# Decode attention with a gated MLP on one core: the value products one tile behind the scores instead of two, with the value tiles loaded one iteration earlier

## The chip, the core and the metric

The kernel runs on one core of a Trainium2 chip. The core's engines run side by side, each through its own list of instructions in order: TensorE (PE, with its weight loads shown as PEld), VectorE (DVE), ScalarE (ACT), GpSimd (POOL) and SyncE (SP). In this kernel SP does one thing: it issues the loads, one after the other, and where a load has to wait for a buffer, every load behind it on SP waits too. The loads run on 16 DMA engines. The metric is the time of one execution in microseconds, lower being better.

## The reference

One decoding step of a transformer block, for 4 sequences of one new token each, width 512, in bf16. Cut to what matters:

```python
x = A_x                                          # (4, 1, 512)
sa, ca, ga, sb, cb, gb = (silu(c) @ w_mod) in 6 parts
h = layernorm(x) * (1 + ca) + sa
q = (h @ wq), 32 heads of 128                    # one query per head and sequence
scores = q . k_cache * 128 ** -0.5               # k_cache: (4, 32, 4096, 128)
o = softmax(scores) . v_cache                    # v_cache: (4, 32, 4096, 128)
x = x + ga * (o @ wo)
h = layernorm(x) * (1 + cb) + sb
x = x + gb * gated_mlp(h)                        # w_in 512 x 1792, gelu, layernorm, gate, w_out 896 x 512
```

Both caches together have 268 MB, and every element is used once. The profile counts 282.73 MB read.

## The kernel before

**Tiles.** The work on the caches is cut into 32 tiles, i = 0 to 31 (the code calls the last one `L`). Tile i is a group g = i // 4 of four heads and a sequence b = i % 4: 4 heads x 4096 keys x 128 numbers, 4096 KB of keys and as much of values. On the chip a tile is 128 partitions x 128 keys x 128 numbers; 32 partitions belong to a head. We write K(i) and V(i) for the loads of its keys and values.

**What one tile needs.** For the scores, DVE multiplies the keys by the query, in two halves of 64 keys per partition (`mult`, L278, written in place into the key tile `kt`). PE adds up groups of 8 products by sixteen matmuls with the identity (`reduce_d`, L284, into `red`), and DVE adds up what is left (`sum8`, L293). `scores` (L298) finishes the second half, finds the maximum over DVE (L302 to L309) and lets ACT take the exponentials (L316), one instruction per head, into one of three buffers `pbd`; the sums come out beside them. `norm_r`, `norm_a` and `norm_b` (L324, L331, L340 or L344) turn these sums into reciprocals: one DVE instruction, one matmul with ones in fp32, which is two passes on PE, and a DVE reciprocal.

The value products are `pv` (L353): 32 matmuls of `pbd` with the value tile `vt` into `ops`, one of two PSUM tiles. `o_pick` (L361, L365) brings the four useful blocks of `ops` together by four DVE instructions, `o_cols` (L375 or L379) turns the result into columns by small matmuls, and `o_scale` (L395) multiplies by the reciprocal. After every fourth tile `project` lets PE multiply by `wo` (`o_proj`, L405), and `add_up` adds the result to `acc` on DVE (L413). The last tile's values go another way, `o_last` (L389): its key tile's shape lets single columns of `pbd` be used, and no `o_pick` is needed.

**Order.** Everything is in the order in which it is written; nothing is planned by a scheduler. Iteration i of the main loop (L433) works on the scores of tile i: `mult(i, 0)`, then `scores(i - 1)`, the norm and the extraction of earlier tiles, `reduce_d(i, 0)`, `mult(i, 1)`, `reduce_d(i, 1)`, and at its end the value products of tile i - 2. The extraction (`o_pick`, `o_cols`, `o_scale`) belongs to tile i - 3. After the loop stand the softmax of tile 31, the extraction of tile 29, the value products and the extraction of tile 30, the projection of tiles 28 to 30, then `o_last`, the second layernorm and the MLP. Of the layernorm and the MLP's first matmul most is done for all columns before the last tile's part is known; the last column is put in behind.

**Buffers and the queue.** `kt` and `vt` have two buffers each. K(i + 2) takes K(i)'s buffer, so its load waits until `reduce_d(i, 1)` has read it; it is issued in iteration i (L455). V(i) takes V(i - 2)'s buffer and is issued at the end of iteration i, behind `pv(i - 2)` (L464 to L466). V(31) takes a key buffer, that of K(30), and comes in four pieces (64, 32, 16 and 16 keys); K(31) comes in two halves. All of these go through SP's queue, with w_mod and wq ahead of them, wo_sb and wo_last issued in iteration 2, and win_sb and wout_sb, the MLP's weights, behind V(31). So the order of the loads is: w_mod, wq, K(0), K(1), V(0), K(2), V(1), K(3), K(4), V(2), wo, K(5), V(3), and so on to K(30), V(28), K(31), V(29), V(30), V(31), win_sb, wout_sb.

The functions that the change touches and what calls them, with the line numbers of the profile:

Of the kernel before, what the change touches and what calls it, by code (L numbers as in the profile page):

```python
# [22 lines left out]
def kernel(  # L23
# [34 lines left out]
    L = NT - 1  # L58
# [12 lines left out]
    def ps_sm(shape, dtype=F32):  # L71
        return psum.tile(shape, dtype, name="sm", bufs=3)
# [18 lines left out]
    def kv_view(cache, i):  # L91
        g, b = divmod(i, B)
        v = cache[b, g * HQ:(g + 1) * HQ].rearrange("h s d -> (h s) d")
        return v.rearrange("(p n) d -> p n d", p=P)
# [3 lines left out]
    def load(dst, src, cuts):  # L98
        n0 = 0
        for n in cuts:  # L100
            nc.sync.dma_start(out=dst[:, n0:n0 + n, :], in_=src[:, n0:n0 + n, :])
            n0 += n
# [6 lines left out]
    def load_v(i):  # L109

        vts[i] = kvp.tile([P, NJ, DH], BF16, name="kt" if i == L else "vt", bufs=2)
        load(vts[i], kv_view(A_v_cache, i), TAIL if i == L else (NJ,))
# [162 lines left out]
    def mult(i, kc):  # L275
        kt = kts[i][:, kc * KC:(kc + 1) * KC, :]
        g, b = divmod(i, B)
        nc.vector.tensor_tensor(out=kt, in0=kt, in1=bc(qbc[:, g, b, :], KC), op=ALU.mult)  # L278
# [19 lines left out]
    def scores(i):  # L298
        sum8(i, 1)
        S = st.pop((i, "S"))  # L300
        mrow = wk.tile([P, 1], F32, name="mrow")
        nc.vector.tensor_reduce(out=mrow, in_=S, axis=AX.X, op=ALU.max)  # L302
        mb = wk.tile([P, R], F32, name="mb")
        nc.vector.tensor_copy(out=mb, in_=mrow.to_broadcast([P, R]))  # L304
        mt = wk.tile([P, R], F32, name="mt")
        nc.vector.transpose(mt, mb)  # L306
        nM = wk.tile([P, 1], F32, name="nM")
        nc.vector.tensor_reduce(out=nM, in_=mt, axis=AX.X, op=ALU.max)  # L308
        nc.vector.tensor_scalar(  # L309
            out=nM, in0=nM, scalar1=-att_scale, scalar2=None, op0=ALU.mult  # L310
        )
        pbd = pbds[i % 3]
        rs = wk.tile([P, 1], F32, name="rs", bufs=3)
        for q in range(HQ):
            r = slice(R * q, R * (q + 1))
            nc.scalar.activation(  # L316
                out=pbd[r, :, q], in_=S[r, :], func=AF.Exp, bias=nM[r, :],
                scale=att_scale, accum_out=rs[r, :],
            )
        st[i, "rs"] = rs  # L320
# [27 lines left out]
    def pv(i):  # L348

        for m in range(NJ // G):  # L350
            n = slice(m * G, (m + 1) * G)
            g = R * (m % 4)
            nc.tensor.matmul(  # L353
                opss[i % 2][g:g + G * HQ], lhsT=pbds[i % 3][:, n, :], rhs=vts[i][:, n, :],
                start=(m < 4), stop=(m >= NJ // G - 4), tile_position=(0, g),
            )

    def o_pick(i):
        ops = opss[i % 2]
        osb = wk.tile([P, DH], F32, name="osb")  # L360
        nc.vector.tensor_scalar(  # L361
            out=osb, in0=ops[:, 0, :], scalar1=selg[:, 0:1], scalar2=None, op0=ALU.mult
        )
        for g in range(1, G):
            nc.vector.scalar_tensor_tensor(  # L365
                out=osb, in0=ops[:, g, :], scalar=selg[:, g:g + 1], in1=osb,
                op0=ALU.mult, op1=ALU.add,
            )
        st[i, "osb"] = osb

    def o_cols(i):
        op = ps_sm([P, 2, 2])
        osb = st.pop((i, "osb"))
        if i // B == NQ - 1:
            nc.tensor.matmul(op, lhsT=osb, rhs=sel4, start=True, stop=True)  # L375
        else:
            for a in range(2):
                for r in range(2):
                    nc.tensor.matmul(  # L379
                        op[64 * a:64 * (a + 1), r, :], lhsT=osb[:, r:P:2],  # L380
                        rhs=sel4[:, a:HQ:2], start=True, stop=True, tile_position=(0, 64 * a),
                    )
        st[i, "op"] = op
# [10 lines left out]
    def o_scale(i):  # L394
        nc.vector.tensor_tensor(  # L395
            out=oTs[:, i], in0=st.pop((i, "op")), in1=st.pop((i, "rz")), op=ALU.mult
        )

    def o_proj(g, b0, b1):
        wp = ps_sm([P, DJ, b1 - b0])  # L400
        for j in range(DJ):
            for q in range(HQ):
                r, t = divmod(q, 2)
                w = wo_last[:, q, :] if g == NQ - 1 else wo_sb[:, g * 2 + t, r, :]
                nc.tensor.matmul(  # L405
                    wp[:, j, :], lhsT=w[:, j:D:DJ], rhs=oTs[:, g * B + b0:g * B + b1, r, t],
                    start=(q == 0), stop=(q == HQ - 1),
                )
        return wp
# [13 lines left out]
    def project(i):  # L423

        if i >= 0 and i % B == BL and i < L:
            adds.append((o_proj(i // B, 0, B), 0, B))
# [6 lines left out]
    for i in range(NT):  # L433
        more = list(QPLAN.get(i, ()))
        mult(i, 0)
        if i >= 1:
            scores(i - 1)
        if i >= 2:
            norm_b(i - 2)
        add_up()  # L440
        if i >= 3:
            o_pick(i - 3)
        reduce_d(i, 0)
        if i >= 3:
            o_cols(i - 3)
        if more:
            queries(more.pop(0))
        mult(i, 1)
        if i >= 1:
            norm_r(i - 1)  # L450
        if i >= 3:
            o_scale(i - 3)
        sum8(i, 0)
        reduce_d(i, 1)
        load_k(i + 2)  # L455
        if i >= 1:
            norm_a(i - 1)
        project(i - 3)
        while more:
            queries(more.pop(0))  # L460
        if i >= 2:
            pv(i - 2)
        if i == 0:
            load_v(1)  # L464
        elif 2 <= i < L:
            load_v(i)  # L466
        if i == 2:
            nc.scalar.dma_start(out=sp_t[:, 0:1], in_=B_w_sp[0:1, 0:1])
            nc.scalar.dma_start(out=sp_t[:, 1:2], in_=B_b_sp.rearrange("(a b) -> a b", b=1))
            mps = ps_sm([P, 3 * DJ, B])  # L470
            mod_cols(2, 3 * DJ, mps)
            nc.vector.tensor_copy(out=modT, in_=mps)
            nc.vector.tensor_copy(out=hcs[:, :, B:2 * B], in_=mps[:, DJ:2 * DJ, :])
            gps = ps_sm([P, P])
            for k in range(DJ):
                for j in range(DJ):
                    nc.tensor.matmul(
                        gps[R * j:R * (j + 1), :], lhsT=cTw[:, k, :],
                        rhs=wm_sb[:, k, 5 * D + j * P:5 * D + (j + 1) * P],
                        start=(k == 0), stop=(k == DJ - 1), tile_position=(0, R * j),  # L480
                    )
            nc.vector.tensor_copy(out=gbr, in_=gps)
            pre_cm.__exit__(None, None, None)
            wts = tl = ctx.enter_context(tc.tile_pool(name="wts", bufs=1))
            wo_sb = wts.tile([P, H // 2 - 2, 2, D], BF16, name="wo_sb")
            wo_last = wts.tile([P, HQ, D], BF16, name="wo_last")
            hl = (H - HQ) * DH
            nc.sync.dma_start(
                out=wo_sb, in_=A_wo[0:hl].rearrange("(t p r) n -> p t r n", p=P, r=2)
            )  # L490
            nc.sync.dma_start(out=wo_last, in_=A_wo[hl:H * DH].rearrange("(q p) n -> p q n", p=P))
        if i == 5:
            sps = ps_sm([P, 2])
            nc.tensor.matmul(sps, lhsT=ones_b, rhs=sp_t, start=True, stop=True)
            nc.vector.tensor_copy(out=spf, in_=sps)
            for k, t in ((0, gbw), (1, gbr)):
                nc.vector.tensor_scalar(
                    out=t, in0=gbr, scalar1=spf[:, k:k + 1], scalar2=None, op0=ALU.mult
                )
            cbT = modT[:, 2 * DJ:3 * DJ, :]  # L500
            nc.vector.tensor_scalar_add(out=cbT, in0=cbT, scalar1=1.0)
        if i == L - 1:
            load_v(L)
            win_sb = wts.tile([P, DJ, F], BF16, name="win_sb")
            nc.sync.dma_start(out=win_sb, in_=B_w_in.rearrange("(p j) n -> p j n", p=P))
            wout_sb = wts.tile([P, NH, D], BF16, name="wout_sb")
            nc.sync.dma_start(out=wout_sb, in_=B_w_out.rearrange("(j p) n -> p j n", p=P))
# [3 lines left out]
    norm_b(L - 1)  # L511
    norm_r(L)
    add_up()
    o_pick(L - 2)
    o_cols(L - 2)
    norm_a(L)
    o_scale(L - 2)
    norm_b(L)
    pv(L - 1)
    o_pick(L - 1)  # L520
    o_cols(L - 1)
    o_scale(L - 1)
# [141 lines left out]
```

## Time and profile before

| what | value |
|---|---|
| median of 3 runs | 675.5 us (673.76 to 675.64) |
| the profiled execution | 673.46 us, its span 671.7 us |
| mean granted clock of TensorE | 0.823 |
| PE busy | 405.1 us (60%) |
| DVE busy | 423.3 us (63%) |
| ACT busy | 85.0 us (13%) |
| HBM read | 282.73 MB, 421 GB/s over the span |
| one multiply of half a key tile on DVE (L278) | 4420 ns |
| one set of 16 matmuls of `reduce_d` | 3.61 us at full clock, 5.04 to 6.56 us where it begins at half clock |

How to read it: the page gives busy times by engine, and cuts the span into 40 slices of 16.8 us, with the busy share of each engine and of the DMA engines in tenths, the granted clock of TensorE (PEclk) and the GB/s moved. "Chain that ended last" follows the work back from the last instruction, at each step to what released it; its shares sum to the span. A row of the timeline has the start and the duration in us, the engine (SPq is a DMA issue on SP), the line, the operation, what it writes and reads, the number of instructions that it merges, and in brackets the idle time of the engine before it with what ended it. Rows of the DMA view end with the median time from the issue of a load to its landing. A row of the windows view has the stretch, its length, the busy time of each engine asked for with its number of instructions, the granted clock, the busy share of the DMA engines and the GB/s.

### The profile page before, as it was taken

How to read it: one execution, taken by the hardware profiler on the slowest of the kernel's cores; microseconds unless marked ns; L12 is line 12 of the kernel's file. 1: busy time of each engine (PE TensorE's matmuls, PEld its weight loads, DVE VectorE, ACT ScalarE, POOL GpSimd, SP SyncE). 2: the span in 40 equal slices, each digit the busy share in tenths (PEclk: the TensorE clock that was granted, in tenths of full speed). 3: DMA queues.
4: the chain of work that ended last, by engine and by line, in shares of the span. 5: the costliest groups of instructions: out<-in, count | busy, mean ns of one | idle time of the engine just before them, and what ended most of it. 6: DMA issues, size and time to landing. Idle time of an engine off the chain costs nothing.

```text
span 671.7 us, 7155 instructions
## 1 busy us (share of the span) xinstructions
PE 405.1 (60%) x2971; PEld 183.0 (27%) x2971; DVE 423.3 (63%) x620; ACT 85.0 (13%) x278; POOL 3.3 (0%) x15
## 2 busy tenths in 40 slices
PE   1185784466577655555666566666556457755766
PEld 1032332222223222222222222223222223322325
DVE  3176593775666777566577666666776566777733
ACT  1012120111011111101111110111111011111112
POOL 1000000000000000000000000000000000000000
PEclk9998988677888777889867777887777898777975
DMA  9999999999999999999999999999999999999994
GB/s 375 437 431 433 422 410 422 434 427 426 434 432 428 433 430 427 434 435 428 426 432 431 435 430 431 425 431 432 432 430 435 426 430 433 433 426 426 436 414 168
DMA packets 13556, 283.19 MB, mean 422 GB/s; under 512 B 1228, under 2 KB 2644, under 8 KB 4692
## 3 DMA queue, kind: packets, MB, share of 16 engines
q1 hardware_dynamic: 13488, 282.73, 98.5%
q8 instruction: 23, 0.38, 0.2%
q14 instruction: 9, 0.07, 0.0%
q10 hardware_dynamic: 36, 0.01, 0.0%
HBM read 282.73 MB, written 0.00 MB: 421 GB/s over the span
## 4 chain that ended last, share of the span: by engine, by line
DMA 53%; DVE 31%; PE 14%; issue 1%; ACT 0%; SPq 0%; DVEq 0%
DMA kt<-in_A_k_cache_dram 53%; DVE kt L278 22%; PE red L284 11%; DVE osb L365 3%; DVE S L293 2%; PE ops L353 1%; DVE osb L361 1%; DVE mrow L302 1%; DVE mt L306 1%; DVE rz L344 1%; PE qps L389 1%; DVE nM L308 0%; DVE mb L304 0%; DVE nM L309 0%; PE sm L185 0%
## 5 line engine op out<-in xcount | busy, mean ns | idle before, releaser
L284 PE MATMUL red<-kt,ident_bf 128*128 128x512 bf16 x1024 | 304.0, 464 | 235.8 <-DVE kt L278 235.8
L278 DVE TENSOR_TENSOR kt<-kt,qbc 128x8192 bf16<-128x8192 bf16 x64 | 282.8, 4420 | 193.6 <-DMA kt<-in_A_k_cache_dram 192.6
L284 PEld LDWEIGHTS <-ident_bf 128*128 128x128 bf16 x1024 | 117.0, 114 | 411.0 <-issue 285.3
L316 ACT ACTIVATE pbd<-S,nM 32x128 bf16<-32x128 f32 x128 | 73.9, 577 | 508.2 <-DVE nM L309 465.2
L353 PE MATMUL ops<-vt,pbd 128*16 128x512 bf16 x992 | 60.3, 386 | 0.0
L293 DVE TENSOR_REDUCE S<-red 128x64 f32<-128x512 f32 x64 | 43.7, 682 | 8.2 <-PE red L284 8.1
L365 DVE SCALAR_TENSOR_TENSOR osb<-ops,selg,osb 128x128 f32<-128x128 f32 x93 | 32.6, 351 | 3.3
L316 ACT ACTIVATION_READ_ACCUMULATOR pbd<-S,nM 32x1 f32 x128 | 32.1, 251 | 0.0
L353 PEld LDWEIGHTS <-pbd 128*16 128x16 bf16 x992 | 22.3, 90 | 23.2 <-issue 1.7
L264 PE MATMUL qps<-wq_sb,hTb 128*32 128x512 bf16 x128 | 9.2, 412 | 9.2 <-DMA wq_sb<-in_A_wq_dram 8.5
L331 PEld LDWEIGHTS sm<-rsb,ones_f 128*128 128x128 f32 x64 | 12.3, 195 | 4.5
L361 DVE TENSOR_SCALAR osb<-ops,selg 128x128 f32<-128x128 f32 x31 | 10.8, 348 | 3.6 <-PE ops L353 2.9
L379 PEld LDWEIGHTS sm<-sel,osb 128*64 128x64 f32 x224 | 9.2, 138 | 11.9 <-issue 11.4
L379 PE MATMUL sm<-sel,osb 128*64 128x2 f32 x224 | 11.6, 205 | 0.0
L268 ACT CAST qbc<-qps 128x512 bf16<-128x512 f32 x8 | 4.7, 585 | 47.8 <-PE qps L264 47.8
L302 DVE TENSOR_REDUCE mrow<-S 128x1 f32<-128x128 f32 x32 | 9.2, 286 | 1.1
L344 DVE RECIPROCAL rz<-sm 64x2 f32<-64x2 f32 x56 | 9.1, 163 | 0.4
L331 PE MATMUL sm<-rsb,ones_f 128*128 128x4 f32 x64 | 9.3, 215 | 0.0
L324 DVE TENSOR_SCALAR rsb<-mask,rs 128x4 f32<-128x4 f32 x32 | 7.2, 224 | 2.4 <-ACT pbd L316 2.4
L306 DVE STREAM_TRANSPOSE mt<-mb 128x32 f32<-128x32 f32 x32 | 6.8, 212 | 1.1
L264 PEld LDWEIGHTS <-hTb 128*32 128x32 bf16 x128 | 3.1, 100 | 13.3 <-issue 10.6
L308 DVE TENSOR_REDUCE nM<-mt 128x1 f32<-128x32 f32 x32 | 6.0, 186 | 1.1
(129 smaller groups left out, 87.6 us busy)
## 6 DMA issues: line engine op xcount, KB each, us to landing
kt<-in_A_k_cache_dram SPq DMA_DIRECT2D x31, 4096.0 KB, 22.9
vt<-in_A_v_cache_dram SPq DMA_DIRECT2D x31, 4096.0 KB, 30.7
wq_sb<-in_A_wq_dram SPq DMA_DIRECT2D x1, 4096.0 KB
kt<-in_A_k_cache_dram SPq DMA_DIRECT2D x2, 2048.0 KB, 20.4
wo_sb<-in_A_wo_dram SPq DMA_DIRECT2D x1, 3584.0 KB
wm_sb<-in_w_mod_dram SPq DMA_DIRECT2D x1, 3072.0 KB
kt<-in_A_v_cache_dram SPq DMA_DIRECT2D x1, 2048.0 KB
win_sb<-in_B_w_in_dram SPq DMA_DIRECT2D x1, 1792.0 KB, 32.7
```

What stands on the lines that cost most here:

```text
L278: nc.vector.tensor_tensor(out=kt, in0=kt, in1=bc(qbc[:, g, b, :], KC), op=ALU.mult)
L284: nc.tensor.matmul(red, lhsT=ident_bf, rhs=kt[:, :, m * RD:(m + 1) * RD], start=(m == 0), stop=(m == DH // RD - 1),)
L293: nc.vector.tensor_reduce(out=st[i, "S"][:, kc * KC:(kc + 1) * KC], in_=st.pop((i, "red", kc)), axis=AX.X, op=ALU.add,)
L302: nc.vector.tensor_reduce(out=mrow, in_=S, axis=AX.X, op=ALU.max)
L306: nc.vector.transpose(mt, mb)
L316: nc.scalar.activation(out=pbd[r, :, q], in_=S[r, :], func=AF.Exp, bias=nM[r, :], scale=att_scale, accum_out=rs[r, :],)
L331: nc.tensor.matmul(z, lhsT=ones_f, rhs=st.pop((i, "rsb")), start=True, stop=True)
L344: nc.vector.reciprocal(out=rz[h, 0, :], in_=z[h, a:HQ:2])
L353: nc.tensor.matmul(opss[i % 2][g:g + G * HQ], lhsT=pbds[i % 3][:, n, :], rhs=vts[i][:, n, :], start=(m < 4), stop=(m >= NJ // G - 4), tile ...
L361: nc.vector.tensor_scalar(out=osb, in0=ops[:, 0, :], scalar1=selg[:, 0:1], scalar2=None, op0=ALU.mult)
L365: nc.vector.scalar_tensor_tensor(out=osb, in0=ops[:, g, :], scalar=selg[:, g:g + 1], in1=osb, op0=ALU.mult, op1=ALU.add,)
L379: nc.tensor.matmul(op[64 * a:64 * (a + 1), r, :], lhsT=osb[:, r:P:2], rhs=sel4[:, a:HQ:2], start=True, stop=True, tile_position=(0, 64 * a),)
```

## The change

The value products of tile i - 1, instead of i - 2, now stand at the end of iteration i, and the extraction and the projection follow one iteration earlier as well. V(i + 1), instead of V(i), is issued behind them. V(1) is issued in iteration 0 as before, and V(2) in iteration 1, where no value tile was issued before. After the loop, the extraction of tile 29 and the value products of tile 30 are gone, since they have run in iteration 31. Buffers, sizes of loads and all instructions stay as they are.

The order of the loads becomes: w_mod, wq, K(0), K(1), V(0), K(2), V(1), K(3), V(2), K(4), V(3), wo, K(5), V(4), and so on to K(30), V(29), K(31), V(30), V(31), win_sb, wout_sb.

```diff
         if i >= 2:
             norm_b(i - 2)
         add_up()
-        if i >= 3:
-            o_pick(i - 3)
+        if i >= 2:
+            o_pick(i - 2)
         reduce_d(i, 0)
-        if i >= 3:
-            o_cols(i - 3)
+        if i >= 2:
+            o_cols(i - 2)
         if more:
             queries(more.pop(0))
         mult(i, 1)
         if i >= 1:
             norm_r(i - 1)
-        if i >= 3:
-            o_scale(i - 3)
+        if i >= 2:
+            o_scale(i - 2)
         sum8(i, 0)
         reduce_d(i, 1)
         load_k(i + 2)
         if i >= 1:
             norm_a(i - 1)
-        project(i - 3)
+        project(i - 2)
         while more:
             queries(more.pop(0))
-        if i >= 2:
-            pv(i - 2)
-        if i == 0:
-            load_v(1)
-        elif 2 <= i < L:
-            load_v(i)
+        if i >= 1:
+            pv(i - 1)
+        if i + 1 < L:
+            load_v(i + 1)
...
     norm_b(L - 1)
     norm_r(L)
     add_up()
-    o_pick(L - 2)
-    o_cols(L - 2)
     norm_a(L)
-    o_scale(L - 2)
     norm_b(L)
-    pv(L - 1)
     o_pick(L - 1)
     o_cols(L - 1)
     o_scale(L - 1)
```

## The prediction

> **What bounds the kernel now.** I read the page first: the slices and the chain of waits.
>
> ```profile
> DMA  9999999999999999999999999999999999999994
> GB/s 375 437 431 433 422 410 422 434 427 426 434 432 428 433 430 427 434 435 428 426 432 431 435 430 431 425 431 432 432 430 435 426 430 433 433 426 426 436 414 168
> ...
> DMA 53%; DVE 31%; PE 14%; issue 1%; ACT 0%; SPq 0%; DVEq 0%
> ```
>
> The DMA engines are full from the first slice to the last but one. Until the last load has landed, time is bytes over rate: a tile of 4096 KB (4.19 MB) at about 430 GB/s is 9.75 us. Reordering loads among themselves saves nothing there; only the stretch behind the last loads, and a hole in the queue, can move the end. DVE and PE stand in the chain because it runs through the release of key buffers, but each key load is issued long before its turn. The list of DMA issues shows it: 22.9 us from issue to landing, 9.75 of them its own, so 13.1 us of other loads lie ahead of it.
>
> ```profile
> kt<-in_A_k_cache_dram SPq DMA_DIRECT2D x31, 4096.0 KB, 22.9
> vt<-in_A_v_cache_dram SPq DMA_DIRECT2D x31, 4096.0 KB, 30.7
> ...
> win_sb<-in_B_w_in_dram SPq DMA_DIRECT2D x1, 1792.0 KB, 32.7
> ...
> wout_sb<-in_B_w_out_dram SPq DMA_DIRECT2D x1, 896.0 KB, 34.8
> ```
>
> Then the end, from the timeline of all engines:
>
> ```profile
> 605.35 0.80 SPq L101 DMA_DIRECT2D kt<-in_A_k_cache_dram  x2
> ...
> 608.87 4.43 DVE L278 TENSOR_TENSOR kt<-kt,qbc 128x8192 bf16<-128x8192 bf16 x1 [6.42 <-DMA kt<-in_A_k_cache_dram]
> ...
> 623.48 4.43 DVE L278 TENSOR_TENSOR kt<-kt,qbc 128x8192 bf16<-128x8192 bf16 x1 [1.78 <-DMA kt<-in_A_k_cache_dram]
> ...
> 631.18 4.42 DVE L278 TENSOR_TENSOR kt<-kt,qbc 128x8192 bf16<-128x8192 bf16 x1
> ...
> 635.65 6.56 PE L284 MATMUL red<-kt,ident_bf 128*128 128x512 bf16 x16 [3.88 <-DVE kt L278]
> ...
> 646.63 0.23 DVE L324 TENSOR_SCALAR rsb<-mask,rs 128x4 f32<-128x4 f32 x1 [2.42 <-ACT pbd L316]
> ...
> 649.30 3.15 PE L353 MATMUL ops<-vt,pbd 128*16 128x512 bf16 x32
> ...
> 652.51 0.35 DVE L361 TENSOR_SCALAR osb<-ops,selg 128x128 f32<-128x128 f32 x1 [2.92 <-PE ops L353]
> ...
> 662.42 1.57 PEld L552 LDWEIGHTS <-win_sb 128*128 128x128 bf16 x56 [0.62 <-DMA win_sb<-in_B_w_in_dram]
> ```
>
> The first half of the last key tile, K(31), lands at 623.48, and from there to the output no engine of the chain waits for a load: two multiplies, the PE sums, the softmax, the products of tile 30 (649.30), their extraction on DVE (652.51), the projection, and the MLP. At 662.4 two things meet: win_sb lands (629.65 issued, 32.7 later is 662.35) and the last column of its operand is ready (662.39). The end is thus bound twice within 0.1 us: by the loads, and by the work behind K(31).
>
> **The change part by part.** Write K(i), V(i) for the loads.
>
> *Order of the queue.* Before: ... K(30) V(28) K(31) V(29) V(30) V(31), win, wout. After: ... K(30) V(29) K(31) V(30) V(31), win, wout, since V(i+1) instead of V(i) follows K(i+2). The bytes are the same, so the last load lands where it did (664.9 for wout). But behind K(31) there is now one tile less, so K(31) lands one tile later. K(30) and K(31)a are 14.61 us apart with one and a half tiles between (9.74 a tile); the move costs **+9.75 us** on K(31)a: 633.2.
>
> *Is that on the path?* DVE waited 1.78 us for K(31)a before; K(30) moves by the same 9.75, so iteration 30 ends at the same distance and DVE waits again. The second half lands about 4.9 us after the first, 3 us before its multiply (7.7 us after). So the chain from 623.48 to the exponentials' end at 646.63 moves whole: 656.4. One accumulation (0.14 us at 629.71) goes one iteration earlier, into DVE's wait: -0.08.
>
> *What leaves the end.* The products of tile 30 now run within iteration 31, right behind the PE sums (before, those of tile 29 ran there, 642.26 to 644.16), beside DVE's softmax; V(30) lands near 648, before them. The extraction of tile 29 (o_pick, four DVE instructions) goes into iteration 31, in the place that tile 28's had. Before, from the start of L324 to the extraction of tile 30 it took 652.51 - 646.63 = 5.88 us. After, what is left is L324 (0.23), the norm's matmul (0.57 at 648.80), its reciprocal (0.18) and three hand-overs of 0.04: 1.1 us. **-4.78 us**. If PE is late with tile 30's products, the extraction waits: its cover is the 4.4 us from the PE sums' end to L324 and the 1.1 us behind it, against 0.4 us for a norm and 3.15 us of products on PE, so 1.9 us is spare.
>
> *Steady state.* V(i+1) is issued behind pv(i-1), in the place where V(i) was behind pv(i-2), 2 us behind K(i+2); on SP nothing else stands behind it until the next K, some 17 us on. pv(i-1) needs V(i-1), next in the queue after K(i), so 9.75 us later; on PE it stands behind two sums, 16 us after K(i). Its probabilities come from exponentials over about 9 us after K(i) (589.31 to 598.0). Zero, hidden by these 6 us; were V later, PE would stall before the next sums, which have idle time (5 to 6 us) before them. The four extractions and the scaling only change their tile. ACT and POOL lose and gain nothing.
>
> *The front.* Iteration 1 gains a set of products (1.9 us) and V(2)'s issue, iteration 2 an extraction (1.5 us); K(4) is then issued near 76.4 instead of 74.9, with K(3) moving until 80 and now V(2) behind it. Zero. The wo loads stand behind one more tile: in the timeline SP's row for wo_last lasted 19.62 us from 80.26, until 99.88, when wo_sb's turn came; that becomes about 109.7, and K(5) is issued behind it. wo_sb and wo_last, 4.19 MB at the 387 GB/s moved from 100 to 105 us, are 10.8 us of cover. If SP were held until wo_sb is through, only wo_last's 1.3 us would cover the start of a load; the output's small DMA takes 2.8 us from issue to the end, so at most 1.5 us of hole. I take 0; a hole cannot be negative, so the ends are 0 and +1.5.
>
> *The clock.* The PE sums at 635.65 took 6.56 us; in the timeline's rows, sums that began at half clock took 5.04 to 6.56, those at full clock 3.61. They follow 3.88 us of PE idle time, as they will after the change, and every row of sums behind a PE gap of over 3 us began at half clock. The ends are the 3.61 of full clock (-2.95) and 6.56 (0); I keep 6.56, the row of the same place. The windows before it, of 3.4 us:
>
> ```profile
> 631.40:634.81 3.41, 0.37 (x3) 1.00 0.98 423
> 634.81:638.22 3.41, 2.57 (x7) 0.50 1.03 442
> ...
> 402.70:406.12 3.42, 1.70 (x14) 0.82 (x13) 3.42 (x1) 0.00 (x0) 0.00 (x0) 1.00 1.00 431
> 406.12:409.53 3.41, 3.27 (x8) 1.13 (x8) 0.89 (x4) 0.00 (x0) 0.00 (x0) 0.50 1.00 432
> ```
>
> The clock fell after a window nearly idle (0.37 us busy), but at 406.12 also after one half busy (1.70 of 3.42). A gap of 3.9 us empties half of some window wherever the windows lie, so half clock is likely again. The Trainium skill (TensorE: Matmul & The Clock Gate, Part 1) says that the clock halves after an idle window of about 3.4 us, in windows that run free of the kernel. By that rule a gap of 3.9 us holds a whole window in one phase of seven, and the sum would mostly be +1.9. The rows with a half-busy window go against it, and they decide.
>
> *Sum.* 9.75 - 0.08 - 4.78 = +4.9, less 0.05 for the wait on win_sb, which lands before its use: **+4.8 us**. On the profiled execution: 673.46 (span 671.7) + 4.8 = 678.3. That execution lies 2.0 under the median of 675.5 (673.76 to 675.64 in the runs shown); on the median it is 680.3. I say 680.0, a little towards the profiled execution, since the terms are its own.
>
> **The rivals.**
> 1. *Full clock in the last sums:* +1.9, 677.4 on the median. For: nearly half of all the sums ran so. Against: those stood behind shorter gaps. 0.04.
> 2. *No change:* K(31) one place on is absorbed. It takes slack of 5 us behind K(31); the chain shows none. 675.5. 0.06.
> 3. *The other side, faster: a quicker stream.* A different neighbour in the queue could make the loads move faster (the slices between the first and the last two range from 410 to 437 GB/s). Everything at the end moves with the stream; 4.8 us is 0.72% of 665 us, so from 430 to 433.1 GB/s the change breaks even, and at 434.5 it is 2 us faster, 673.5. Against: every load keeps its size and pieces. 0.03. The 4.78 us taken from the end cannot by themselves make it faster, since win_sb lands at 662.35 either way.
> 4. *A hole at the wo loads:* +1.5 more, 681.8. 0.04.
> 5. *K(31) still later, or tile 30's products late as well:* above 682. 0.03.
>
> The forecast has 0.80.
>
> **How the numbers follow.** A measurement of this kernel tells about 0.3% (2.0 us) from no change. Low end: full clock, 677.4, less 1.0 for half the spread of the runs (673.5 to 675.6), 676.4; high end: the hole, 681.8, and half of that 1.0, 682.3. Faster: rival 3, 0.03. Same: rival 2 and most of rival 1, 0.09. Slower: the rest, 0.88.
>
> **What would show it.** Right: the DMA slices full to the end as now; K(31)a's multiply near 633 with the last load still near 665; the last sums behind it; products of tile 30 before the exponentials end; extraction of tile 30 about 1.1 us after L324, near 657.4; the first win_sb matmul near 667 with its weights long landed; so about 11.6 us from the last load to the end of the span instead of 6.8. Wrong: K(31) landing less than a tile later, a DVE wait other than for K(31)a in iteration 31, last sums of 3.6 us, a dip in the GB/s near 110 to 120 us, or a span set by win_sb.

## The result and the profile after

The changed kernel takes 677.52 us in the median of 7 runs (677.11 to 678.64), the kernel before 674.8 us in the median of 7 (673.76 to 675.64). The ratio is 1.0046, with a 95% interval of 1.0037 to 1.0056: slower by 2.7 us between the medians, and by 2.5 to 3.8 us over the interval. The profiled execution took 677.11 us with a span of 675.3, against 673.46 and 671.7: 3.6 us more.

The page of the changed kernel, slices and chain:

```profile
DMA  9999999999999999999999999999999999999992
GB/s 373 435 430 434 432 431 395 427 430 433 430 435 428 435 430 430 433 431 428 431 432 430 435 426 433 430 429 432 431 432 430 431 433 432 429 428 428 437 406 79
...
DMA 56%; DVE 29%; PE 13%; issue 1%; ACT 0%; SPq 0%; DVEq 0%
```

The loads run as before. The slow stretch of the wo loads (410 and 422 GB/s in the sixth and seventh slice before, 431 and 395 now) has moved with them. Otherwise only the last slice differs much: 79 GB/s instead of 168. The list of DMA issues, with the time from issue to landing, and the timeline's issues of the same two loads:

```profile
win_sb<-in_B_w_in_dram SPq DMA_DIRECT2D x1, 1792.0 KB, 25.9
...
wout_sb<-in_B_w_out_dram SPq DMA_DIRECT2D x1, 896.0 KB, 28.0
```

```profile
636.35 0.43 SPq L503 DMA_DIRECT2D win_sb<-in_B_w_in_dram  x1
636.83 0.43 SPq L505 DMA_DIRECT2D wout_sb<-in_B_w_out_dram  x1
```

The last load lands at 636.83 + 28.0 = 664.83, where it landed before (664.93). So all of the 3.6 us lie behind the loads. The timeline of the end, all engines:

```profile
633.38 4.43 DVE L278 TENSOR_TENSOR kt<-kt,qbc 128x8192 bf16<-128x8192 bf16 x1 [1.72 <-DMA kt<-in_A_k_cache_dram]
...
641.00 4.41 DVE L278 TENSOR_TENSOR kt<-kt,qbc 128x8192 bf16<-128x8192 bf16 x1
...
645.47 5.30 PE L284 MATMUL red<-kt,ident_bf 128*128 128x512 bf16 x16 [3.88 <-DVE kt L278]
...
650.81 1.91 PE L353 MATMUL ops<-vt,pbd 128*16 128x512 bf16 x32
...
655.19 0.23 DVE L324 TENSOR_SCALAR rsb<-mask,rs 128x4 f32<-128x4 f32 x1 [2.41 <-ACT pbd L316]
...
656.06 0.32 DVE L361 TENSOR_SCALAR osb<-ops,selg 128x128 f32<-128x128 f32 x1
...
666.10 1.63 PE L546 MATMUL qps<-hcs,win_sb 128*128 128x8 bf16 x56 [0.53 <-DVE hcs L539]
```

DVE waits 1.72 us for the first half of K(31), as it did before, but at 633.38 instead of 623.48. The products of tile 30 (650.81) run while DVE is at the softmax, and their extraction starts 0.87 us after L324 instead of 5.88. The first MLP matmul starts at 666.10 and waited for its operand `hcs`, no longer for win_sb, which had landed at 662.25.

### The profile page after: what moved, and what is told of

The parts are those of the page before. It is cut to its first block, busy times and chain, and to the rows that moved or that the text cites. A ratio compares the mean times of both kernels' runs of the same rounds, so it can differ in the third digit from the quotient of the medians.

```text
span 675.3 us, 7151 instructions
## 1 busy us (share of the span) xinstructions
PE 403.7 (60%) x2971; PEld 182.7 (27%) x2971; DVE 423.0 (63%) x620; ACT 85.0 (13%) x278; POOL 3.3 (0%) x15
## 4 chain that ended last, share of the span: by engine, by line
DMA 56%; DVE 29%; PE 13%; issue 1%; ACT 0%; SPq 0%; DVEq 0%
DMA kt<-in_A_k_cache_dram 56%; DVE kt L278 21%; PE red L284 11%; DVE osb L365 3%; DVE S L293 1%; DVE osb L361 1%; DVE mrow L302 1%; DVE mt L306 1%; DVE rz L344 1%; PE qps L389 1%; DVE nM L308 0%; DVE mb L304 0%; DVE nM L309 0%; PE sm L185 0%; ACT pbd L316 0%
## 5 line engine op out<-in xcount | busy, mean ns | idle before, releaser
L284 PE MATMUL red<-kt,ident_bf 128*128 128x512 bf16 x1024 | 304.3, 464 | 242.1 <-DVE kt L278 242.1
L284 PEld LDWEIGHTS <-ident_bf 128*128 128x128 bf16 x1024 | 116.9, 114 | 417.9 <-issue 290.5
L324 DVE TENSOR_SCALAR rsb<-mask,rs 128x4 f32<-128x4 f32 x32 | 7.2, 223 | 2.4 <-ACT pbd L316 2.4
```

Of the source, the lines that this page charges most:

```text
L284: nc.tensor.matmul(red, lhsT=ident_bf, rhs=kt[:, :, m * RD:(m + 1) * RD], start=(m == 0), stop=(m == DH // RD - 1),)
```

## The experiments

The theory: the time hangs on the place of the last keys in the queue, less the work that leaves the end; the front, the steady state and the products' being one behind cost nothing. The rivals: a hole in the queue at the wo loads, late products in the steady state, or slack behind K(31).

**K(31) one place later, and nothing else.**

```diff
@@ the kernel before, in the main loop
-        load_k(i + 2)
+        if i + 2 != L:
+            load_k(i + 2)
...
         elif 2 <= i < L:
             load_v(i)
+        if i + 2 == L:
+            load_k(L)
```

> The kernel before, its products two tiles behind, with one thing changed: K(31) is issued behind V(29), so it has the place that the change gives it. Theory (the end hangs on K(31)'s landing): its first half lands 9.75 us later, near 633, nothing is taken from the end, and the time is 8.2 to 9.7 us above before (the lower where the last PE sums take 5.0 us instead of 6.56). Rival (K(31) has slack, the change's cost comes from the front or the steady state): within 2 us of before.

Measured: 681.64 us (680.36 to 682.42, 4 runs), ratio to before 1.0104 (1.0085 to 1.0123): 7.0 us slower by the ratio, 6.8 between the medians. The place of K(31) alone costs more than the whole change, and the rival falls. But it is 1.2 us less than the low end of what the theory expected. Its timeline:

```profile
634.97 4.43 DVE L278 TENSOR_TENSOR kt<-kt,qbc 128x8192 bf16<-128x8192 bf16 x1 [11.50 <-DMA kt<-in_A_k_cache_dram]
639.45 6.30 PE L284 MATMUL red<-kt,ident_bf 128*128 128x512 bf16 x16 [10.64 <-DVE kt L278]
...
647.14 3.61 PE L284 MATMUL red<-kt,ident_bf 128*128 128x512 bf16 x16 [1.27 <-DVE kt L278]
...
655.18 0.23 DVE L324 TENSOR_SCALAR rsb<-mask,rs 128x4 f32<-128x4 f32 x1 [2.41 <-ACT pbd L316]
...
657.88 3.59 PE L353 MATMUL ops<-vt,pbd 128*16 128x512 bf16 x32
...
661.53 0.35 DVE L361 TENSOR_SCALAR osb<-ops,selg 128x128 f32<-128x128 f32 x1 [3.36 <-PE ops L353]
```

K(31) is 11.49 us later than in the first profile of before. In this execution the stream was late already ahead of it: the multiply of K(30), which also waits for its load, began at 610.63, against 608.87, 1.76 us later. So 9.73 us are the place in the queue, one tile. What was not expected: DVE and PE idle over 10 us for K(31), so the first of the two PE sums of iteration 31 began at half clock and took 6.30 us, which left a gap of only 1.27 us before the last sums, and these ran at full clock: 3.61 us instead of 6.56. From L324 to the extraction it takes 6.35 us, where before took 5.88. With the late stream taken out, 9.73 - 2.95 + 0.47 = 7.25, against a span longer by 8.9 - 1.76 = 7.1.

**Half of the delay.** K(31) between the two halves of V(29).

```diff
@@ the kernel before, load_v
+        if i == L - 2:
+            src = kv_view(A_v_cache, i)
+            nc.sync.dma_start(out=vts[i][:, 0:KC, :], in_=src[:, 0:KC, :])
+            load_k(L)
+            nc.sync.dma_start(out=vts[i][:, KC:NJ, :], in_=src[:, KC:NJ, :])
+            return
@@ in the main loop
-        load_k(i + 2)
+        if i + 2 != L:
+            load_k(i + 2)
```

> The kernel before with K(31) issued between the two halves of V(29): half of the delay. Theory: the first half of K(31) lands 4.9 us later, near 628.4, and the time is 3.4 to 4.9 us above before. Rival (K(31) has some slack and only a part of the tile counts): under 2 us.

Measured: 676.93 us (676.43 to 678.17, 6 runs), ratio 1.0036 (1.0022 to 1.005): 2.4 us slower by the ratio, 2.0 between the medians, again below the theory's low end. The interval, 1.5 to 3.4 us, reaches below the rival's bound of 2 us, so the time alone does not decide. The profile does (the added lines move the line numbers by six: L284 is the multiply here, L290 the PE sums):

```profile
634.85 6.55 PE L290 MATMUL red<-kt,ident_bf 128*128 128x512 bf16 x16 [5.79 <-DVE kt L284]
...
642.54 3.61 PE L290 MATMUL red<-kt,ident_bf 128*128 128x512 bf16 x16 [1.02 <-DVE kt L284]
```

It is the same cause: first sums at half clock, a short gap, last sums at full clock. With K(30) 2.01 us late in this execution (610.88), K(31)'s place accounts for 4.88 of the 6.89 us by which its multiply is later (630.37), half a tile; 4.88 - 2.95 + 0.47 = 2.4, and the extraction of tile 30 is later by 656.93 - 652.51 - 2.01 = 2.4. Both kernels get the same gain from the clock, and between them lie 4.7 us of the medians for half a tile, where half of 9.75 is 4.9. So no part of the second half of the delay vanishes in slack; of the first half, at most the 0.7 us by which a second profile of before (below) has the work ready ahead of win_sb.

**The change in the first half only.** Up to tile 15 as changed, then as before.

```diff
@@ the kernel before, in the main loop
+    SW = 15
+    picks, done = [], []
     for i in range(NT):
+        picks, done = done, []
...
-        if i >= 3:
-            o_pick(i - 3)
+        for j in picks:
+            o_pick(j)
...
-        if i >= 2:
-            pv(i - 2)
-        if i == 0:
-            load_v(1)
-        elif 2 <= i < L:
+        if 1 <= i <= SW:
+            done.append(i - 1)
+        elif i >= SW + 2:
+            done.append(i - 2)
+        for j in done:
+            pv(j)
+        if i <= SW:
+            load_v(i + 1)
+        elif SW + 2 <= i < L:
             load_v(i)
```

(`o_cols`, `o_scale` and `project` run over `picks` as well.)

> The change up to tile 15, the kernel before from there on: products one behind and values one iteration ahead in the first half, with the wo loads held on SP as in the changed kernel, then one iteration without products, and the order of the queue and the end as before. Theory: the front and the steady state cost nothing, the DMA engines stay full, K(31) lands near 623.5: within 0.3% of before. Rival (the cost is a hole at the wo loads or late products in the steady state): 1.5 to 3.5 us above before.

Measured: 674.77 us (673.9 to 675.42, 10 runs), ratio 1.0001 (0.9991 to 1.001). K(31)'s multiply begins at 623.50, and the last sums took 4.91 us. The front, with SP held at wo_last for 27.88 us instead of 19.62, and 15 iterations of the new steady state cost nothing that can be measured: the interval allows -0.6 to +0.7 us.

**The changed kernel again.** No edit, beside the others on each of two chips.

> The changed kernel once more, as the reference beside the others: 2.5 to 4 us above before, its last PE sums between 5.0 and 6.6 us.

> The changed kernel, as the reference beside the others: 2.5 to 4 us above before.

Measured: 677.04 us (676.92 to 677.13, 4 runs), ratio 1.0038 (1.0023 to 1.0053), and 677.88 us (677.35 to 678.53, 4 runs), ratio 1.0051 (1.0037 to 1.0064). The last sums took 4.99 and 5.30 us.

The first of these two ran on the same chip as the kernel with K(31) a tile later (681.64), where K(31) has the same place in the queue but nothing leaves the end. The changed kernel is 4.6 us faster. In the profiles it takes 32.60 us from K(31)'s multiply to the first MLP matmul, against 36.43: from L324 to the extraction 1.07 instead of 6.35, and last sums of 4.99 instead of 3.61. So the work that leaves the end is gained in full: 5.3 us in these two profiles, less 1.4 for the slower sums.

**The changed kernel with PE kept busy.** Sixteen matmuls into a PSUM tile that nothing reads, in PE's gap before the last sums.

```diff
@@ the changed kernel, in the main loop
         sum8(i, 0)
+        if i == L:
+            dummy = ps_q()
+            for _ in range(16):
+                nc.tensor.matmul(
+                    dummy, lhsT=ident_bf, rhs=qbc[:, 0:GQ, 0, :], start=True, stop=True
+                )
         reduce_d(i, 1)
```

> The changed kernel with 16 matmuls of no use put on PE between the two sums of iteration 31, in the 3.88 us in which it waits for DVE. Theory: the last sums then run at full clock, 3.6 us instead of 5.30 (5.0 to 6.6 over the runs), and since they are on the path, the time falls by 1.5 to 2.5 us against the changed kernel, to 0.5 to 2 us above before. Rival (the clock in this place is off the path, or the matmuls hold up the sums): no change, or up to 1 us slower than the changed kernel.

Measured: 675.51 us (675.28 to 675.74, 11 runs), ratio to before 1.0015 (1.0006 to 1.0024). Against the changed kernel's run on the same chip (677.88) it is 2.4 us faster, in the profile 675.5 - 673.5 = 2.0, of which 0.3 is K(31) landing earlier in this execution. The timeline:

```profile
645.34 3.61 PE L284 MATMUL red<-kt,ident_bf 128*128 128x512 bf16 x16 [0.41 <-DVE kt L278]
...
653.38 0.23 DVE L324 TENSOR_SCALAR rsb<-mask,rs 128x4 f32<-128x4 f32 x1 [2.41 <-ACT pbd L316]
...
654.24 0.32 DVE L361 TENSOR_SCALAR osb<-ops,selg 128x128 f32<-128x128 f32 x1
```

The last sums fall from 5.30 to 3.61 us, and the whole end moves up by these 1.7 us: the clock is on the path here, and paid in full. win_sb landed at 662.11 and its first matmul ran at 664.28, so even now the work behind K(31) sets the end.

**The kernel before with less work behind K(31).** The same sixteen matmuls, and the extraction of tile 29 ahead of the norm of tile 31.

```diff
@@ the kernel before, in the main loop: the 16 matmuls, as above
@@ after the loop
     norm_b(L - 1)
-    norm_r(L)
-    add_up()
     o_pick(L - 2)
     o_cols(L - 2)
-    norm_a(L)
     o_scale(L - 2)
+    norm_r(L)
+    add_up()
+    norm_a(L)
     norm_b(L)
```

> The kernel before with two things done to the work behind K(31): the same 16 matmuls keep PE busy, so that the last sums take 3.6 instead of 6.56 us, and the extraction of tile 29 stands ahead of the norm of tile 31, in the time in which DVE waits for the exponentials, which takes about 1.3 us from the way to tile 30's products. Theory (the end is bound twice, by win_sb's landing as well): the work is up to 4.3 us earlier and then waits for win_sb; the time falls by 0 to 0.3 us. Rival (only the work behind K(31) sets the end): 3 to 4.3 us faster than before.

Measured: 674.08 us (673.5 to 675.78, 11 runs), ratio 0.9999 (0.999 to 1.0008): nothing. The timeline:

```profile
635.93 3.61 PE L284 MATMUL red<-kt,ident_bf 128*128 128x512 bf16 x16 [0.41 <-DVE kt L278]
...
643.97 0.23 DVE L324 TENSOR_SCALAR rsb<-mask,rs 128x4 f32<-128x4 f32 x1 [0.21 <-ACT pbd L316]
...
648.29 3.59 PE L353 MATMUL ops<-vt,pbd 128*16 128x512 bf16 x32 [3.65 <-DMA vt<-in_A_v_cache_dram]
...
662.54 1.65 PE L558 MATMUL qps<-hcs,win_sb 128*128 128x8 bf16 x56 [1.01 <-DMA win_sb<-in_B_w_in_dram]
```

L324 comes 2.66 us earlier than in the first profile of before, and the gain is lost at two loads: the products of tile 30 wait 3.65 us for V(30), and the first MLP matmul waits 1.01 us for win_sb. The loads bound the kernel before at its end, not the work behind K(31).

**The kernel before again.**

> The kernel before once more, for a second profile: 673.5 to 676 us, win_sb's landing and the work behind K(31) within 1 us of one another, the last PE sums anywhere from 5.0 to 6.6 us.

Measured: 673.53 us, span 671.8.

```profile
636.09 4.97 PE L284 MATMUL red<-kt,ident_bf 128*128 128x512 bf16 x16 [3.88 <-DVE kt L278]
...
662.50 1.66 PE L552 MATMUL qps<-hcs,win_sb 128*128 128x8 bf16 x56 [1.28 <-DMA win_sb<-in_B_w_in_dram]
```

The last sums took 4.97 us here, 1.6 less than in the first profile, and the span is the same within 0.1 us: the MLP waited for win_sb. So the clock of the last sums is free before the change, and paid after it.

**The products one behind, with the keys' order turned back.** K(31) ahead of V(29) again; tiles 29 and 30 have their products in iteration 31.

```diff
@@ the changed kernel, in the main loop (o_pick, o_cols and o_scale run for 2 <= i < L)
+        if i == L - 2:
+            load_v(L - 2)
+        if i == L:
+            pv(L - 2)
-        if i >= 1:
+        if i >= 1 and i != L - 1:
             pv(i - 1)
-        if i + 1 < L:
+        if i + 1 < L and i != L - 3:
             load_v(i + 1)
@@ after the loop
     norm_b(L - 1)
+    o_pick(L - 2)
+    o_cols(L - 2)
+    o_scale(L - 2)
     norm_r(L)
```

> The changed kernel with the order of the queue at the end turned back: K(30), K(31), V(29), V(30), V(31). Products stay one behind up to tile 28; those of tile 29 and 30 both run in iteration 31, and the extraction of tile 29 stands in DVE's wait for the exponentials. K(30) still lands a tile later than before (618.5), K(31) right behind it, so DVE goes from iteration 30 to 31 without a wait, near 631.5 instead of 633.4, and its second multiply comes near 637.7 instead of 641. Theory (the change costs time only by the last keys' place, and the loads bound the rest): the work behind K(31) is done before win_sb lands, and the time is within 0.3% of before. Rival (it is products one behind as such that cost): as the changed kernel, 2.5 to 4 us above before.

Measured: 674.15 us (673.85 to 675.62, 10 runs), ratio 1.0 (0.999 to 1.001).

```profile
631.65 4.42 DVE L278 TENSOR_TENSOR kt<-kt,qbc 128x8192 bf16<-128x8192 bf16 x1
...
637.87 4.39 DVE L278 TENSOR_TENSOR kt<-kt,qbc 128x8192 bf16<-128x8192 bf16 x1
...
642.31 3.61 PE L284 MATMUL red<-kt,ident_bf 128*128 128x512 bf16 x16 [2.58 <-DVE kt L278]
...
663.07 1.66 PE L553 MATMUL qps<-hcs,win_sb 128*128 128x8 bf16 x56 [1.64 <-DMA win_sb<-in_B_w_in_dram]
```

DVE goes from tile 30 to tile 31 without a wait, and the MLP waits for win_sb again. With the change's steady state up to tile 28 and the last keys in their old order, the cost is gone. The rival, that products one behind cost something as such, falls. The clock has a share in this: the gap before the last sums is 2.58 us here, and they ran at full clock. Sums of 5.30 us would have used up the 1.64 us by which the work is ahead of win_sb, so the second multiply, 3.1 us earlier than in the changed kernel (637.87 against 641.00), removes the cost only just in that case.

No kernel tried is faster than the kernel before. Those that are as fast (the first-half kernel, the shortened one and the last one) all end at win_sb. V(31) stands right ahead of it, so no order of these loads brings win_sb earlier without delaying V(31); whether that pays was not tried.

The key times of all profiles, in us:

| kernel | K(31)'s first multiply | last sums took | L324 | extraction of tile 30 | win_sb lands | first MLP matmul | span |
|---|---|---|---|---|---|---|---|
| before | 623.48 | 6.56 | 646.63 | 652.51 | 662.35 | 662.44 | 671.7 |
| before again | 623.93 | 4.97 | 645.49 | 651.89 | 662.40 | 662.50 | 671.8 |
| before, shortened | 623.76 | 3.61 | 643.97 | 651.93 | 662.49 | 662.54 | 671.8 |
| first half changed | 623.50 | 4.91 | 645.01 | 651.96 | 662.80 | 662.88 | 672.1 |
| keys' order turned back | 631.65 | 3.61 | 650.65 | 651.51 | 663.03 | 663.07 | 672.3 |
| after | 633.38 | 5.30 | 655.19 | 656.06 | 662.25 | 666.10 | 675.3 |
| after, again | 633.30 | 4.99 | 654.80 | 655.87 | 662.37 | 665.90 | 675.1 |
| after, again (second chip) | 633.55 | 5.30 | 655.36 | 656.23 | 662.35 | 666.25 | 675.5 |
| after, PE kept busy | 633.25 | 3.61 | 653.38 | 654.24 | 662.11 | 664.28 | 673.5 |
| K(31) half a tile later | 630.37 | 3.61 | 650.58 | 656.93 | 664.08 | 667.06 | 676.4 |
| K(31) a tile later | 634.97 | 3.61 | 655.18 | 661.53 | 663.82 | 671.40 | 680.6 |

From the first MLP matmul to the end of the span it is 9.2 to 9.3 us in every row. That matmul starts at the later of two things: win_sb's landing, in the first five rows (in the very first, the work was ready within 0.1 us of it), or the work behind K(31), in the other six.

## Why the prediction was right, and which terms were off

The direction was right: slower, by the place of the last keys, less what leaves the end. The forecast was +4.8 us; the profiled executions lie 3.6 apart, the medians 2.7 (the interval of the ratio is 2.5 to 3.8 us). The forecast of 680.0 is 2.5 above the 677.52 measured: 1.2 of it is in the terms, the rest in the step from the profiled execution to the median.

- *K(31) a tile later, +9.75:* it was 9.90 (633.38 against 623.48), and DVE waited for it as before (1.72 us against 1.78). Right.
- *What leaves the end, -4.78:* from L324 to the extraction 0.87 us are left of 5.88, so -5.01; the norm's matmul took 0.36 us instead of 0.57. Right.
- *The steady state, 0, and the front, 0:* the DMA slices are full, SP's row for wo_last ended at 81.69 + 27.91 = 109.60 (109.7 was forecast), and the first-half kernel is within 0.1% of before. Right.
- *The clock, 0 (6.56 kept on both sides):* this is the term that was mis-sized. That the last sums begin at half clock was right. But they took 5.30 us in the profile and 4.99 and 5.30 in the other two: 1.3 to 1.6 less than forecast. The row of the same place was one sample, the longest of its kind; the mean of the 34 sums that took over 5 us in the profile of before, 5.75 us, would have been nearer. Worse, it was taken to cancel between the two kernels. It does not: before the change these sums are not on the path, as 4.97 us with an unchanged span shows.
- *"The end is bound twice within 0.1 us":* half right. In the profile shown the two met; in the second one win_sb was later by 0.7 us than the work (the last column of its operand was ready at 661.70, the landing at 662.40). The shortened kernel shows which of the two binds: with its L324 2.66 us earlier, nothing was gained. The loads bind, and in the profiles taken the work behind K(31) was level or a little ahead.
- *Sum:* 9.90 - 0.08 - 5.01 - 1.26 = 3.55, and 0.11 more from the extraction to the first MLP matmul (10.04 us against 9.93): 3.66, where the spans differ by 3.6.
- *The step from the profiled execution to the median, +2.0:* the profiled execution of before was low among its runs (1.3 us under the median of the seven), that of after less so (0.4). The forecast carried 1.7 of the 2.0 over to the changed kernel, and 0.4 was there. What sets the spread of before's runs was not settled.

Of the rivals, full clock in the last sums was put at +1.9, 677.4 on the median. The 677.52 measured is next to that, so the number alone would speak for this rival; it came about by a mis-sized clock term and a mis-sized step to the median together, and that the range held it owes something to luck. The traces speak against the rival: the last sums began at half clock every time, as the gap of 3.88 us said they would, in both profiles of before, in all three of the changed kernel, and in the first-half kernel. With PE kept busy, full clock was there, and it came to +1.8 in the profiles (673.5 against 671.7) and to +1.1 between the medians (675.51 against 674.38). The Trainium skill (TensorE: Matmul & The Clock Gate, Part 1) lets the clock halve after an idle window of about 3.4 us; by an estimate from that figure a gap of 3.88 us holds such a window in one phase of seven, so most of the six would have begun at full clock. None did. No change, a quicker stream, a hole at the wo loads and late products of tile 30 did not come.

## What to carry to other kernels

In a kernel that the loads fill from end to end, look for the last input whose processing is long, and count the bytes behind it in the queue: each tile moved from behind it to ahead of it makes it land later by a whole transfer time (9.7 to 9.9 us here). The kernel pays for that as soon as the work behind the input is longer than the loads that are left, less what the work itself gains: 7.0 us for a tile moved alone, 2.7 us where 5.0 us of work left the end with it. Bringing one stream forward in a shared queue always puts another back; here values that were not urgent went ahead of keys that were. And a duration that varies from run to run must not be cancelled between two kernels before it is known that both have it on their path.

## What the runs showed of the hardware

- The PE clock turns a delay into a gain in part. Waiting 10.64 us for K(31) made the first sums slow (6.30 us), which closed the gap before the last ones (1.27 us) and let them run at full clock (3.61). So a tile's delay cost 7.0 us instead of 9.75.
- The granted clock follows how busy PE was in windows of fixed length. Cut from 27.22 us on into 188 windows of 3.4135 us, the profile of before has one granted clock in each of them, 1.00 or 0.50. From 33 us on, a window at full clock in which PE was busy for less than 0.46 of the time was followed by one at half clock, 31 times out of 31, and one busier than 0.51 never was; a window at half clock was followed by one at full clock from 0.86 on, with one exception, and never up to 0.76. The profile of the changed kernel shows the same with a wider border, 0.42 to 0.59. That would explain the six of six: a gap of 3.88 us takes at least its half, 1.94 us, out of one window, which leaves that window busy for 0.43 at most.
- A key tile can land 1.9 us later in one execution than in another, and a lag can shrink again. Up to K(30), the kernel with K(31) a tile later has the loads of the kernel before. The first multiplies of its tiles, which wait for the landing, begin later than there by 1.57 us for tile 5 (121.86 against 120.29), 0.40 for tile 28 (570.27 against 569.87) and 1.88 for tile 29 (591.19 against 589.31). What moves them was not found.
- Of the kernels with ten or more runs, the changed one with PE kept busy is the steadiest: 11 runs within 0.46 us (675.28 to 675.74), where the shortened kernel before, on the same chip, spreads over 2.3 us (673.5 to 675.78), and the changed kernel without the sixteen matmuls over 1.2 us in four runs. Its end hangs on K(31)'s landing and a fixed chain, the shortened one's on the last loads. That the landing of the last loads varies between executions would explain the one, and the length of the last sums at half clock the other; neither was tried.
